# Semaphores between VectorE's two-port operations and GpSimd's adds, all shifts on GpSimd, new buffer rings, and score phases of distinct row groups

## Chip, cores, metric

One core of one Trainium2 chip. The metric is the device time of one execution in microseconds (us), compared in runs of the same chip. The experiments ran in three calls on three chips, each beside the kernel before on the same chip; where kernels of different calls are compared, the ratio to before is the fair measure and a difference of medians is only near it.

## The reference

```python
def _A_ref(x, wq, wk, wv, wo):                    # 32 heads of 16, one shared key/value head
    q = (x @ wq).reshape(B, S, 32, 16).transpose(0, 2, 1, 3)
    k, v = x @ wk, x @ wv                         # S = 2048, D = 512
    p = _softmax(einsum("bhqd,bkd->bhqk", q, k) * 16 ** -0.5)
    return einsum("bhqk,bkd->bhqd", p, v).transpose(0, 2, 1, 3).reshape(B, S, 512) @ wo
# ...
xn = _layernorm(A_x)
s = _A_ref(xn, ...)
g = _silu(silu(xn @ B_w1) @ B_w2)                 # 512 -> 1792 -> 512
return A_x + s * g
```

Attention dominates: 2048 score tiles of 128 keys x 512 queries (32 head groups of 64 tiles) must each pass an exponential and be multiplied by V.

## The kernel before

The kernel plans all engines at build time: a small scheduler places every operation on a modelled clock, and what comes out is one fixed order of instructions per engine, with semaphore waits for data hazards. The chip then runs those orders; only the waits react to real durations.

A score tile is a 32-row matmul. Up to four of them, in four different row groups of the array, form one "score phase" and run side by side. A tile then takes one of two ways.

- Exact: ScalarE computes exp out of PSUM, two neighbouring banks per instruction where it can (128x1024), else one (128x512).
- Approximate: VectorE writes `a*x + b` as uint16, which read as bf16 is a rough exp (Schraudolph's trick). Four such tiles form a batch (`db_sb`). Three more copies of the batch, with 32, 64 and 96 added to the bit patterns (`ds_sb`, the "shifts"), are weighted into V, so that the errors cancel. An approximated tile so costs four products with V instead of one.

Products with V are 32-column matmuls, four side by side (a "round"), accumulated in one PSUM bank. When a head group is complete, VectorE transposes the bank, takes reciprocals and multiplies.

A shift can be done by either engine; the scheduler withdraws the other's task once one is placed:

```python
whole[DV] = pl.add(Task(DV, T_SH, lambda v: v.tensor_scalar(           # 128x2048 uint16
    ds_sb[:, s, :], db_sb[:, bt.b, :], SHIFT[j - 1], 1.0, op0=ALU.add, op1=ALU.mult),
    reads, ds_keys(s), lambda: URGENT if urgent() else 6, list(bt.P.values()),
    on_place=lambda op: placed(op, DV), ports=2,
    gate=lambda: urgent() or len(shifts) >= DV_MIN))                   # DV_MIN = 4
whole[PO] = pl.add(Task(PO, T_P64, lambda g: g.int64_add(              # four uint16 in one word
    ds_sb[:, s, :].bitcast(U64), db_sb[:, bt.b, :].bitcast(U64), words),
    reads, ds_keys(s), lambda: 5 if urgent() else 6, list(bt.P.values()),
    on_place=lambda op: placed(op, PO), ports=2))
```

`ports=2` marks operations that use the pair of SBUF ports that VectorE shares with GpSimd: VectorE's shifts, the normalising multiply (`otr_sb`), the last residual add (`ob_sb`), and every GpSimd add. In the plan they exclude each other, on the chip nothing says so:

```python
def locked(self, eng, ports):
    if ports != 2 or eng not in self.lock:
        return 0.0
    return self.lock[PO if eng == DV else DV]    # end of the other's last one, in the plan only
# ...
NDB, NDS = 7, 6          # batch and shift buffers;  NPA, PRESS = 26, 20: exp tiles
NMIN = 2                 # a score phase may have two matmuls
t3 = pl.add(Task(DV, 332.0, ... v.tensor_tensor(o3, f3, rcp.to_broadcast(...), ALU.mult),
    [("F", k), ("rcp", k)], [("otr", oi % 2, e)], 3, [t2, ...], ports=2))        # priority 3
```

The softmax here doesn't subtract the row's maximum and nothing guards it: scores larger than these inputs give would overflow.

## Time and profile before

| | before |
|---|---|
| time, median of 3 | 695.43 us |
| span of the profiled run | 693.2 us |
| score phases / of them with two matmuls / doubled row groups | 649 / 101 / 14 |
| rounds of 32-column matmuls | 1677 |
| double / single exps | 600 / 148 |
| approximated tiles; shifts on GpSimd / VectorE | 700; 489 / 36 |

The counts below the line are of the built program. The page of the kernel before: first the busy time of each engine with its share and number of instructions, then groups of instructions (line, engine, operation, output <- input, count | busy us, mean ns of one | idle time before, and what ended it).

```profile
PE 670.8 (97%) x8843; PEld 193.8 (28%) x8843; DVE 627.9 (91%) x1088; ACT 667.4 (96%) x827; POOL 519.5 (75%) x500
...
L1341 ACT ACTIVATE pa_sb<-ps 128x1024 bf16<-128x1024 f32 (+1 forms) x748 | 639.7, 980 | 7.4 <-PE ps L776 6.3
L1019 POOL INT64_ADD ds_sb<-db_sb x489 | 515.5, 1072 | 158.9 <-DVE db_sb L962 102.9
L962 DVE TENSOR_SCALAR db_sb<-ps 128x512 uint16<-128x512 f32 x700 | 449.9, 682 | 44.1 <-PE ps L776 40.0
...
L1014 DVE TENSOR_SCALAR ds_sb<-db_sb 128x2048 uint16<-128x2048 uint16 x36 | 37.3, 1039 | 0.1
...
L1100 DVE TENSOR_TENSOR otr_sb<-f_sb,rcp_sb 128x256 bf16<-128x256 f32 x32 | 19.0, 595 | 0.2
```

ScalarE and TensorE are both 96 to 97% busy. A mean can mix two shapes or two situations: start-to-start, a double exp takes 0.904 us and a single one 0.477 when nothing holds it. Split by whether a GpSimd add overlaps them in time, the 36 VectorE shifts took 0.696 us alone (3 of them) and 1.07 beside an add (33, up to 1.60); the multiply 0.417 alone (7) and 0.645 beside an add (25, up to 1.26).

The list of waits of the kernel before (engine, what waited <- for whom: us in total, times, longest). The first line also holds the idle time that the engine shows at every change from rounds to a score phase, 0.425 us in the median of all 649, so only what is longer is lateness:

```profile
PEld ps L776 <- DVE db_sb L962: 104.1, 227, 1.2
POOL ds_sb L1019 <- DVE db_sb L962: 102.9, 69, 34.1
...
POOL ds_sb L1019 <- PE ps L1079: 55.2, 34, 5.3
...
PEld ps L1079 <- DVE ds_sb L1014: 3.2, 5, 1.3
...
PE ps L1079 <- DVE f_sb L1096: 2.8, 6, 0.6
```

### The profile page before, as it was taken

The page shows a single profiled execution, that of the slowest core. Times are in us where ns is not written, and L with a number is a line of the kernel's source. Part 1 is how long each engine was busy: PE and PEld are TensorE (multiplying, and loading weights), DVE is VectorE, ACT ScalarE, POOL GpSimd, SP SyncE. Part 2 cuts the span into 40 slices and gives each one's busy share as a digit, 9 for nine tenths or more (in the row PEclk, how much of TensorE's full clock was granted, in tenths as well). Part 3 has the DMA queues.
Part 4 walks back from the last instruction along what each step waited for, and adds up shares of the span by engine and source line. Part 5 has one row for each costly group of instructions (what it writes and reads, how often), then busy time and mean ns, then how long its engine had stood idle before and what let it go on. Part 6 is the DMA issues. An engine that isn't in the chain of part 4 may idle for free.

```text
span 693.2 us, 20821 instructions
## 1 busy us (share of the span) xinstructions
PE 670.8 (97%) x8843; PEld 193.8 (28%) x8843; DVE 627.9 (91%) x1088; ACT 667.4 (96%) x827; POOL 519.5 (75%) x500
## 2 busy tenths in 40 slices
PE   8899999999999999999999999999999999999995
PEld 4422222222222222222222222222222222222221
DVE  9889989989998999989998999989899988999994
ACT  4899999999999999999999999999999999999994
POOL 2067887797897778877698676788789677888891
PEclk9999999999999999999999999999999999999999
DMA  9310000000000000000000100000000000000000
GB/s 302 127 18 1 3 2 2 1 3 2 2 2 17 18 32 2 2 2 2 1 2 2 32 18 17 1 2 3 2 2 1 17 18 24 9 2 2 2 2 31
DMA packets 11435, 12.64 MB, mean 18 GB/s; under 512 B 1808, under 2 KB 10768, under 8 KB 11344
## 3 DMA queue, kind: packets, MB, share of 16 engines
q1 hardware_dynamic: 10288, 11.28, 5.1%
q8 instruction: 71, 1.16, 0.7%
q10 hardware_dynamic: 1056, 0.03, 0.1%
q14 instruction: 20, 0.16, 0.1%
HBM read 8.95 MB, written 2.10 MB: 16 GB/s over the span
## 4 chain that ended last, share of the span: by engine, by line
PE 62%; ACT 24%; DVE 12%; issue 1%; ACTq 0%; DVEq 0%
PE ps L1079 25%; ACT pa_sb L1341 23%; PE ps L776 21%; PE ps L466 15%; DVE db_sb L962 5%; DVE ds_sb L1014 2%; ACT t_sb L588 1%; DVE stats_sb L413 1%; DVE f_sb L1096 1%; DVE ob_sb L643 1%; DVE u_sb L590 0%; DVE otr_sb L1100 0%; DVE xn_sb L442 0%; DVE fin_sb L640 0%; DVE xnT_sb L493 0%
## 5 line engine op out<-in xcount | busy, mean ns | idle before, releaser
L1341 ACT ACTIVATE pa_sb<-ps 128x1024 bf16<-128x1024 f32 (+1 forms) x748 | 639.7, 980 | 7.4 <-PE ps L776 6.3
L1019 POOL INT64_ADD ds_sb<-db_sb x489 | 515.5, 1072 | 158.9 <-DVE db_sb L962 102.9
L962 DVE TENSOR_SCALAR db_sb<-ps 128x512 uint16<-128x512 f32 x700 | 449.9, 682 | 44.1 <-PE ps L776 40.0
L776 PE MATMUL ps<-qt_sb,kt_sb 32*128 32x512 bf16 x2048 | 257.4, 384 | 9.1 <-DVE db_sb L962 4.0
L1079 PE MATMUL ps<-ds_sb,v_sb 128*32 128x512 bf16 x2100 | 265.1, 383 | 0.2
L1079 PE MATMUL ps<-pa_sb,v_sb 128*32 128x512 bf16 x1348 | 242.8, 383 | 1.8 <-DVE ds_sb L1014 1.0
L1079 PE MATMUL ps<-db_sb,v_sb 128*32 128x512 bf16 x700 | 171.0, 383 | 2.8 <-DVE f_sb L1096 2.8
L776 PEld LDWEIGHTS ps<-qt_sb,kt_sb 32*128 32x128 bf16 x2048 | 63.9, 91 | 281.6 <-ACT pa_sb L1341 145.8
L1079 PEld LDWEIGHTS ps<-ds_sb,v_sb 128*32 128x32 bf16 x2100 | 65.9, 95 | 60.7 <-issue 40.0
L1079 PEld LDWEIGHTS ps<-pa_sb,v_sb 128*32 128x32 bf16 x1348 | 61.2, 95 | 45.1 <-issue 23.6
L466 PE MATMUL ps<-xnT_sb,w_sb 128*32 128x512 bf16 x896 | 73.1, 384 | 0.2 <-DVE db_sb L962 0.2
L466 PE MATMUL ps<-w_sb,u_sb 128*32 128x512 bf16 x896 | 69.6, 384 | 0.0
L1079 PEld LDWEIGHTS ps<-db_sb,v_sb 128*32 128x32 bf16 x700 | 42.6, 95 | 25.8 <-issue 13.3
L588 ACT ACTIVATE t_sb<-ps 128x512 bf16<-128x512 f32 x72 | 46.3, 643 | 0.0
L590 DVE SCALAR_TENSOR_TENSOR u_sb<-t_sb,ps 128x512 bf16<-128x512 bf16 x56 | 38.1, 681 | 4.5 <-ACT t_sb L588 4.0
L1014 DVE TENSOR_SCALAR ds_sb<-db_sb 128x2048 uint16<-128x2048 uint16 x36 | 37.3, 1039 | 0.1
L1096 DVE STREAM_TRANSPOSE f_sb<-ps 128x512 f32<-128x512 f32 x32 | 22.7, 708 | 7.5 <-PE ps L1079 7.4
L466 PEld LDWEIGHTS ps<-xnT_sb,w_sb 128*32 128x32 bf16 x896 | 16.7, 94 | 25.0 <-issue 18.3
L466 PEld LDWEIGHTS ps<-w_sb,u_sb 128*32 128x32 bf16 x896 | 16.2, 94 | 26.3 <-issue 22.8
L466 PE MATMUL ps<-wo_sb,on_sb 128*32 128x512 bf16 x256 | 20.4, 383 | 0.1
L466 PE MATMUL ps<-xnT_sb,wq_sb 128*32 128x512 bf16 x256 | 20.3, 383 | 0.0
L1100 DVE TENSOR_TENSOR otr_sb<-f_sb,rcp_sb 128x256 bf16<-128x256 f32 x32 | 19.0, 595 | 0.2
(53 smaller groups left out, 153.3 us busy)
## 6 DMA issues: line engine op xcount, KB each, us to landing
w_sb<-in_B_w_dram SPq DMA_DIRECT2D x2, 1792.0 KB, 13.1
xr_sb<-in_A_x_dram SPq DMA_DIRECT2D x16, 128.0 KB, 2.6
out_dram<-ob_sb SPq DMA_DIRECT2D x16, 128.0 KB, 1.7
ds_sb<-in_A_x_dram SPq DMA_DIRECT2D x3, 512.0 KB, 7.2
ds_sb<-in_A_x_dram SPq DMA_DIRECT2D x4, 128.0 KB, 2.6
wq_sb<-in_A_wq_dram SPq DMA_DIRECT2D x1, 512.0 KB, 5.2
wo_sb<-in_A_wo_dram SPq DMA_DIRECT2D x1, 512.0 KB, 16.0
kt_sb<-kt_sb SPq DMA_DIRECT2D x4, 64.0 KB, 2.3
```

What stands on the lines that cost most here:

```text
L413: ts_ = pl.add(Task(DV, 593.0, lambda v, t=t: v.bn_stats(stats_sb[:, t, :], x_tile(t)), [xkey(t)], [("st", t)], 1 + j, gate=(lambda: q_don ...
L466: last = h.matmul(bank(b)[32 * j:32 * (j + 1), 0:n], lhsT=lhs(j), rhs=rhs, start=start, stop=stop, tile_position=(0, 32 * j), skip_group_c ...
L588: t1 = Task(AC, 490.0, lambda a: a.activation(t_sb[:, k, :], src, ACT.Tanh, scale=scale), [held], [("t", k)], 0, [t0])
L590: t2 = Task(DV, T_P, lambda v: v.scalar_tensor_tensor(out=dst, in0=t_sb[:, k, :], scalar=1.0, in1=src, op0=ALU.add, op1=ALU.mult), [held, ...
L776: return pe.matmul(bank(b), lhsT=kt_sb[32 * i:32 * i + 32, g % 2, kt * P:(kt + 1) * P], rhs=qt_sb[32 * i:32 * i + 32, (g // 2) % NQR, :], ...
L962: bt.P[i] = pl.add(Task(DV, T_P, lambda v, b=b, i=i, bb=bt.b: v.tensor_scalar(db_sb[:, bb, i * NQ:(i + 1) * NQ], bank(b), 128.0 * LOG2E, 1 ...
L1014: whole[DV] = pl.add(Task(DV, T_SH, lambda v: v.tensor_scalar(ds_sb[:, s, :], db_sb[:, bt.b, :], SHIFT[j - 1], 1.0, op0=ALU.add, op1=ALU.m ...
L1019: whole[PO] = pl.add(Task(PO, T_P64, lambda g: g.int64_add(ds_sb[:, s, :].bitcast(U64), db_sb[:, bt.b, :].bitcast(U64), words), reads, ds_ ...
L1079: h = pe.matmul(bank(OB)[32 * i:32 * (i + 1), :], lhsT=lhs, rhs=rhs, start=s0, stop=s1, tile_position=(0, 32 * i), skip_group_check=True)
L1096: t1 = pl.add(Task(DV, T_TR, lambda v: v.transpose(f_sb[:, k, :], bank(OB)), [("ps", OB)], [("F", k)], 1, [norm.get(("m", g - 2))]))
L1100: t3 = pl.add(Task(DV, 332.0, lambda v: v.tensor_tensor(o3[:, :, val:val + DH], f3[:, :, val:val + DH], rcp_sb[:, k, :].unsqueeze(2).to_br ...
L1341: op = pl.place(AC, 0.8333 * NQ * n + T_AF, lambda a: a.activation(pa_sb[:, s * NQ:(s + n) * NQ].rearrange("p (b n) -> p b n", n=NQ), ps3[ ...
```

## The change

Intent: make the exclusion real with semaphores, so that a two-port operation of one engine never blocks inside the other's; take the shifts off VectorE altogether; let GpSimd stand back when a VectorE two-port operation is about to be ready, and place that one first; and choose the row groups of a score phase distinct, three or four at a time. SBUF moves from exp tiles and batches to shift buffers.

```diff
-T_P64, DV_MIN, T_LIB = 1035.0, 4, 300.0
+T_P64, DV_MIN, T_LIB = 1035.0, 40, 300.0          # 40 is never reached: no VectorE shift
+HOLD_PO, URG_SPLIT = 300.0, 0                     # nor when urgent
-NEAR, AHEAD = 24, 0.6
+NEAR, AHEAD = 12, 0.6
-NPA, PRESS = 26, 20
+NPA, PRESS = 22, 16
+NDB, NDS = 6, 8                                   # were 7, 6
-WIDE, NMIN, EARLY = 2, 2, 200.0
+WIDE, NMIN, EARLY = 2, 3, 200.0
# place(): a real dependency on the other engine's last two-port operation
+        other = self.last2.get(PO if eng == DV else DV) if ports == 2 and eng in self.last2 else None
+        if other is not None:
+            deps.append(other)
# avail(): GpSimd stands back
+        if task.eng == PO and task.ports == 2:
+            for d in self.tasks[DV]:
+                if d.ports == 2 and d.gate is None and all(p.op is not None for p in d.preds) and (
+                        self.ready(DV, d.reads, d.writes) <= self.clk[PO] + HOLD_PO):
+                    return None
# the multiply and the residual add come first
-  [("F", k), ("rcp", k)], [("otr", oi % 2, e)], 3, ...
+  [("F", k), ("rcp", k)], [("otr", oi % 2, e)], -1, ...
# pick_a(): a row group already used in the phase is taken again only if nothing else is left
-  if len(res) < n and a_left(gg, i) > 0 and (i not in used or len(used) == 4 or gg == g and nleft[gg] <= 4):
+  if len(res) < n and a_left(gg, i) > 0 and (i not in used or not strict and not res):
# (cut: release of a batch per quarter, splitting code that stays unused with NPIECE = 1; in the
# plan the exclusion now ends when the other engine can see the semaphore, not when the operation ends)
```

The built program has 657 score phases (1 doubled row group, none of two matmuls), 1676 rounds, 652 double and 32 single exps, 712 approximated tiles and 534 GpSimd adds.

More of the change, by code (lines that the diff above doesn't have):

```diff
@@ L22 @@
 T_P, T_SH, T_TR, T_AF = 600.0, 600.0, 630.0, 64.3
-T_P64, DV_MIN, T_LIB = 1035.0, 4, 300.0
+T_P64, DV_MIN, T_LIB = 1035.0, 40, 300.0
+NPIECE = 1
+HOLD_PO, URG_SPLIT = 300.0, 0
 RSQRT_M = float(0x5F1FFFF9)
@@ L50 @@
 CLOSING, URGENT = 3, 1.5
-NPA, PRESS = 26, 20
+NPA, PRESS = 22, 16
+NDB, NDS = 6, 8
+STOL4 = 0.0
 START_Z, START_H = 8, 14
 EVAC = ()
-WIDE, NMIN, EARLY = 2, 2, 200.0
+WIDE, NMIN, EARLY = 2, 3, 200.0
 ONE_LIMIT = 2500.0
@@ L92, in __init__ @@
         self.dma_t = self.acc_t = 0.0
-        self.lock = {DV: 0.0, PO: 0.0}
+        self.last2 = {DV: None, PO: None}
     def vis(self, op, eng):
@@ L138, in place @@
         op.end = t0 + dur
-        if eng in self.lock and ports == 2:
-            self.lock[eng] = op.end
+        if eng in self.last2 and ports == 2:
+            self.last2[eng] = op
         op.dma, op.ring = dma, None
@@ L161, in locked @@
     def locked(self, eng, ports):
-        if ports != 2 or eng not in self.lock:
+        if ports != 2 or eng not in self.last2:
             return 0.0
-        return self.lock[PO if eng == DV else DV]
+        other = self.last2[PO if eng == DV else DV]
+        return 0.0 if other is None else self.vis(other, eng)
     def add(self, task):
@@ L295, in bass_recurrent_scan__grouped_kv_mqa__dense_activation_silu__prompt_kernel @@
     BANKS = (0, 1, 2, 3, 4, 5, 7)
-    NDB, NDS = 7, 6
     NQR, NON = 4, 2 * NOC
@@ L643, in final @@
             t2 = Task(DV, 333.0, lambda v: v.tensor_tensor(ob_sb[:, tt % 4, :], fin_sb[:, k, :], xr_sb[:, tt % 4, :], ALU.add),
-                      [("fin", k), ("xr", tt % 4)], [("ob", tt % 4)], 1, [t1, xr_task[tt], out_task.get(tt - 4)], ports=2)
+                      [("fin", k), ("xr", tt % 4)], [("ob", tt % 4)], -1, [t1, xr_task[tt], out_task.get(tt - 4)], ports=2)
             t3 = Task(SP, 60.0, lambda e: e.dma_start(of.rearrange("(t p) d -> p t d", p=P)[:, tt, :], ob_sb[:, tt % 4, :]),
@@ L811, in d_batch @@
             bt = Job()
-            bt.g, bt.slots, bt.b, bt.P, bt.nsh, bt.left = g, {}, free[0], {}, 0, K + 3
+            bt.g, bt.slots, bt.b, bt.P, bt.nsh, bt.left = g, {}, free[0], {}, 0, 4 * K
             return bt
@@ L816, in pick_a @@
             res = []
-            used = set()
+            used = set(avoid)
             g = a_group(0)
             st["gA"] = g
-            for gg in (g, g + 1):
-                if gg >= NG:
-                    break
-                order = sorted(range(4), key=lambda i: (i in avoid and gg == g, -a_left(gg, i), i))
-                again = True
-                while len(res) < n and again:
-                    again = False
-                    for i in order:
-                        if len(res) < n and a_left(gg, i) > 0 and (i not in used or len(used) == 4 or gg == g and nleft[gg] <= 4):
-                            if not slot_ok(gg, i):
-                                return None if not res else res
-                            res.append((gg, i, take(gg, i)))
-                            used.add(i)
-                            again = True
+            for strict in (True, False):
+                for gg in (g, g + 1):
+                    if gg >= NG:
+                        break
+                    again = True
+                    while len(res) < n and again:
+                        again = False
+                        for i in sorted(range(4), key=lambda i: (-a_left(gg, i), i)):
+                            if len(res) < n and a_left(gg, i) > 0 and (i not in used or not strict and not res):
+                                if not slot_ok(gg, i):
+                                    return None if not res else res
+                                res.append((gg, i, take(gg, i)))
+                                used.add(i)
+                                again = True
             return res
@@ L854, in s_phase_ready @@
             n = min(n, 4)
-            while n > NMIN and bt[n - 1][0] > need:
+            while n > NMIN and bt[n - 1][0] > need + STOL4:
                 n -= 1
@@ L993, in bass_recurrent_scan__grouped_kv_mqa__dense_activation_silu__prompt_kernel, with ready @@
         shifts = []
-        shifts = []
         def split(bt, s, j):
-            whole = {}
-            def placed(pop, eng):
-                other = DV if eng == PO else PO
-                pl.tasks[other].remove(whole[other])
-                shifts.remove(whole)
-                release(bt)
-                for i in range(4):
+            whole = {"po": []}
+            width = 4 // NPIECE
+            def ready(pop, slots):
+                for i in slots:
+                    release(bt)
                     kt = bt.slots[i]
@@ L1008, in placed, with placed_dv, placed_po @@
                                          [("Ds", s, i)] + v_reads(j, kt), ("s", s)))
+            def placed_dv(pop):
+                for t in whole["po"]:
+                    pl.tasks[PO].remove(t)
+                shifts.remove(whole)
+                ready(pop, range(4))
+            def placed_po(pop, k):
+                if whole[DV] is not None:
+                    pl.tasks[DV].remove(whole[DV])
+                    whole[DV] = None
+                    shifts.remove(whole)
+                ready(pop, range(k * width, (k + 1) * width))
             reads = [("Db", bt.b, i) for i in range(4)]
@@ L1016, in split @@
                 reads, ds_keys(s), lambda: URGENT if urgent() else 6, list(bt.P.values()),
-                on_place=lambda op: placed(op, DV), ports=2,
-                gate=lambda: urgent() or len(shifts) >= DV_MIN))
-            whole[PO] = pl.add(Task(PO, T_P64, lambda g: g.int64_add(
-                ds_sb[:, s, :].bitcast(U64), db_sb[:, bt.b, :].bitcast(U64), words),
-                reads, ds_keys(s), lambda: 5 if urgent() else 6, list(bt.P.values()),
-                on_place=lambda op: placed(op, PO), ports=2))
+                on_place=placed_dv, ports=2, gate=lambda: URG_SPLIT and urgent() or len(shifts) >= DV_MIN))
+            for k in range(NPIECE):
+                cols = slice(k * width * NQ, (k + 1) * width * NQ)
+                whole["po"].append(pl.add(Task(PO, T_P64, lambda g, cols=cols: g.int64_add(
+                    ds_sb[:, s, cols].bitcast(U64), db_sb[:, bt.b, cols].bitcast(U64), words),
+                    reads[k * width:(k + 1) * width], ds_keys(s)[k * width:(k + 1) * width],
+                    lambda: 5 if urgent() else 6, list(bt.P.values()),
+                    on_place=lambda op, k=k: placed_po(op, k), ports=2)))
             shifts.append(whole)
@@ L1102, in make_norm @@
                 rcp_sb[:, k, :].unsqueeze(2).to_broadcast([P, NQ // 32, DH]), ALU.mult),
-                [("F", k), ("rcp", k)], [("otr", oi % 2, e)], 3, [t2, t2_task.get(oi - 2)], ports=2))
+                [("F", k), ("rcp", k)], [("otr", oi % 2, e)], -1, [t2, t2_task.get(oi - 2)], ports=2))
             norm[("m", g)] = t3
```

## The prediction

> **What bounds the kernel now.** Two engines at once. The busy table has ScalarE at 96%, TensorE at 97%, VectorE 91%, GpSimd 75%. From the first exp at 13.1 us to the last at 683.8 (timeline) ScalarE runs back to back: a double-bank exp steps every 0.904 us, a single one or a tanh every 0.477. Minimum steps: 600×0.904 + 148×0.477 + 72×0.477 = 647 us; 23 us of those 671 are stalls. TensorE repeats "score phase, then k rounds of four 32-column matmuls": 0.868 us with two rounds, 0.217 for each more, so 0.435 for a score phase with its two mode switches. 649 phases, 1677 rounds and 14 doubled row groups make about 648 us; stalls again 23 us. By the list of waits the largest excess of TensorE's idle time is behind VectorE: late Schraudolph evictions 8 us, transpose 3.4, VectorE shifts 2, gating 1.4.
>
> VectorE is late partly because of collisions: a VectorE shift takes 0.696 us alone, 1.07 mean (up to 1.6) while a GpSimd shift runs; the normalising multiply 0.417 alone, 0.645 beside one, up to 1.26. GpSimd adds take 1.039 alone and 1.19 beside two-port VectorE work. This agrees with the Trainium skill, "SBUF — State Buffer", Who interferes with whom: the second op on the shared port pair fully blocks.
>
> **What the change does** (instruction counts of the built programs).
> - VectorE: 36 shifts leave (37.3 us), 12 evictions come (+7 us); 48 multiplies and adds wait on a semaphore instead of blocking inside. Net −30 to −35 us of occupancy.
> - GpSimd: 489→534 adds, +45×1.02 = +46 us, less the 16 us lost to collisions; about 80% busy.
> - ScalarE: double exps 600→652, singles 148→32: +47.0 −55.3 = −8.3 us.
> - TensorE: 649→657 score phases (+3.5 us), doubled row groups 14→1 (−2.8), rounds 1677→1676. Net +0.5 us.
>
> **Critical path.** ScalarE's demand falls to 639 us, TensorE's stays at 648, so TensorE becomes the sole limit. The gain is what TensorE's 23 us of stalls lose, of which about 15 lie behind VectorE. I expect 7 to 11 us of them to go: VectorE is lighter and never surprised by a blocked shift; ScalarE is nearly 9 us looser. The rest stays: PSUM holds only about two phases ahead, so the mix of two-, three- and four-round cycles still makes each engine wait for the other. Start (13 us) and tail (11 us) hardly move.
>
> **Predicted time: 686 us** (−1.4%), 8 in 10 between 677 and 694. Faster by over 2%: 0.20; within 2%: 0.78; slower by over 2%: 0.02.
>
> **What would show it.** Right: the normalising multiply at 0.42 mean and the output add near 0.41, no spread; every GpSimd add at 1.04; VectorE busy near 590 us; ScalarE busy near 650–655 with more idle before exp; TensorE still 97%, its excess waits behind evictions about 4 us. Wrong: VectorE idle before the multiplies on GpSimd of more than 15 us, passed on to score phases; GpSimd above 90%; TensorE waiting for shifts where VectorE no longer helps; exp waiting for free ring slots (22 instead of 26).
>
> **What would make it wrong.** If TensorE's stalls come from the alternation with ScalarE and not from late VectorE work, little is gained (about 692). If plan and chip agree so much better that stalls nearly vanish, it is near 677. If the semaphores chain a VectorE delay into GpSimd and back, it is no faster.

## More of the kernel before

The evictions (L962), which read PSUM, took 0.682 beside adds and 0.683 alone.

GpSimd waits for work or for a free shift buffer, and for no two-port operation of VectorE: there is no semaphore to wait for.

## The result

| | before | after |
|---|---|---|
| time, median of 4 | 695.49 us | 685.14 us |
| ratio, 95% interval | 1 | 0.9849 [0.9832, 0.9866] |
| span of the profiled run | 693.2 | 684.2 |
| first exp / last exp end / span end | 13.1 / 683.8 / 693.2 | 13.3 / 674.8 / 684.2 |
| TensorE excess over minimum cycles | 24.3 | 12.4 |
| ScalarE excess over minimum steps | 23.2 | 22.1 |

Ratios here and below are the mean time of one kernel's fast runs over that of the other's of the same rounds, so not quite the ratio of the medians. "TensorE excess" sums, over all score phases, the time to the next one less 0.868 us (two rounds) less 0.217 for each further round (rounds counted in the trace, four matmuls to a round). Doubled row groups are in it: at an estimated 0.217 each, 3.0 of the 24.3 and 0.2 of the 12.4. "ScalarE excess" sums start-to-start steps from the first exp to the last, less 0.904 (double exp) and 0.477 (single exp, tanh).

The page of the changed kernel:

```profile
PE 668.1 (98%) x8887; PEld 191.7 (28%) x8887; DVE 603.0 (88%) x1064; ACT 658.8 (96%) x763; POOL 548.8 (80%) x545
...
L1042 POOL INT64_ADD ds_sb<-db_sb x534 | 544.9, 1040 | 117.8 <-DVE db_sb L975 65.2
L1365 ACT ACTIVATE pa_sb<-ps 128x1024 bf16<-128x1024 f32 (+1 forms) x684 | 630.5, 1027 | 6.8 <-PE ps L789 6.3
L975 DVE TENSOR_SCALAR db_sb<-ps 128x512 uint16<-128x512 f32 x712 | 468.6, 684 | 61.4 <-PE ps L789 57.7
...
L1124 DVE TENSOR_TENSOR otr_sb<-f_sb,rcp_sb 128x256 bf16<-128x256 f32 x32 | 13.3, 417 | 0.3
```

The multiply now takes 0.417 on average, and GpSimd's adds 1.040. ScalarE runs 684 exps where it ran 748. The list of waits of the changed kernel:

```profile
PEld ps L789 <- DVE db_sb L975: 80.0, 178, 0.7
...
POOL ds_sb L1042 <- DVE db_sb L975: 65.2, 48, 32.5
...
POOL ds_sb L1042 <- DVE otr_sb L1124: 32.3, 29, 2.2
POOL ds_sb L1042 <- PE ps L1103: 10.4, 13, 2.8
POOL ds_sb L1042 <- DVE ob_sb L656: 9.3, 10, 1.1
```

The new lines are the third and the fifth: GpSimd waits 32.3 us for the multiply and 9.3 us for the residual add. VectorE hardly waits for GpSimd at all. TensorE's wait behind evictions fell from 104.1 us in 227 waits to 80.0 in 178; taking 0.43 off each wait that is longer than 0.46, the excess fell from 8.2 to 4.2 us. By the same count, over PEld and PE together, the waits before rounds behind the transpose fell from 2.6 to 1.1 and those behind VectorE's shifts from 1.7 to nothing.

### The profile page after: what moved, and what is told of

It reads as the page before. It is cut to its first block, busy times and chain, and to the rows that moved or that the text cites. A ratio compares the mean times of both kernels' runs of the same rounds, so it can differ in the third digit from the quotient of the medians.

```text
span 684.2 us, 21033 instructions
## 1 busy us (share of the span) xinstructions
PE 668.1 (98%) x8887; PEld 191.7 (28%) x8887; DVE 603.0 (88%) x1064; ACT 658.8 (96%) x763; POOL 548.8 (80%) x545
## 4 chain that ended last, share of the span: by engine, by line
PE 54%; ACT 35%; DVE 9%; issue 1%; DMA 1%; SPq 0%; DVEq 0%
ACT pa_sb L1365 33%; PE ps L1103 22%; PE ps L789 19%; PE ps L479 14%; DVE db_sb L975 4%; ACT t_sb L601 2%; DVE stats_sb L426 1%; DVE f_sb L1120 1%; DVE u_sb L603 1%; DMA ds_sb<-in_A_x_dram 1%; DVE xn_sb L455 0%; DVE otr_sb L1124 0%; DVE xnT_sb L506 0%; DVE tmp_sb L603 0%; SPq L373 0%
## 5 line engine op out<-in xcount | busy, mean ns | idle before, releaser
L1042 POOL INT64_ADD ds_sb<-db_sb x534 | 544.9, 1040 | 117.8 <-DVE db_sb L975 65.2
L1365 ACT ACTIVATE pa_sb<-ps 128x1024 bf16<-128x1024 f32 (+1 forms) x684 | 630.5, 1027 | 6.8 <-PE ps L789 6.3
L975 DVE TENSOR_SCALAR db_sb<-ps 128x512 uint16<-128x512 f32 x712 | 468.6, 684 | 61.4 <-PE ps L789 57.7
L1103 PE MATMUL ps<-ds_sb,v_sb 128*32 128x512 bf16 x2136 | 277.5, 383 | 0.0
L1103 PE MATMUL ps<-db_sb,v_sb 128*32 128x512 bf16 x712 | 186.5, 384 | 1.1 <-DVE f_sb L1120 1.1
L1103 PEld LDWEIGHTS ps<-ds_sb,v_sb 128*32 128x32 bf16 x2136 | 69.1, 95 | 54.0 <-issue 35.3
L479 PE MATMUL ps<-w_sb,u_sb 128*32 128x512 bf16 x896 | 73.1, 384 | 0.0
L1103 PEld LDWEIGHTS ps<-db_sb,v_sb 128*32 128x32 bf16 x712 | 46.3, 95 | 22.3 <-issue 14.5
L1124 DVE TENSOR_TENSOR otr_sb<-f_sb,rcp_sb 128x256 bf16<-128x256 f32 x32 | 13.3, 417 | 0.3
L603 DVE SCALAR_TENSOR_TENSOR tmp_sb<-t_sb,ps 128x512 bf16<-128x512 bf16 x16 | 10.8, 677 | 2.0 <-ACT t_sb L601 1.9
```

Of the source, the lines that this page charges most:

```text
L479: last = h.matmul(bank(b)[32 * j:32 * (j + 1), 0:n], lhsT=lhs(j), rhs=rhs, start=start, stop=stop, tile_position=(0, 32 * j), skip_group_c ...
L603: t2 = Task(DV, T_P, lambda v: v.scalar_tensor_tensor(out=dst, in0=t_sb[:, k, :], scalar=1.0, in1=src, op0=ALU.add, op1=ALU.mult), [held, ...
L975: bt.P[i] = pl.add(Task(DV, T_P, lambda v, b=b, i=i, bb=bt.b: v.tensor_scalar(db_sb[:, bb, i * NQ:(i + 1) * NQ], bank(b), 128.0 * LOG2E, 1 ...
L1042: whole["po"].append(pl.add(Task(PO, T_P64, lambda g, cols=cols: g.int64_add(ds_sb[:, s, cols].bitcast(U64), db_sb[:, bt.b, cols].bitcast( ...
L1103: h = pe.matmul(bank(OB)[32 * i:32 * (i + 1), :], lhsT=lhs, rhs=rhs, start=s0, stop=s1, tile_position=(0, 32 * i), skip_group_check=True)
L1124: t3 = pl.add(Task(DV, 332.0, lambda v: v.tensor_tensor(o3[:, :, val:val + DH], f3[:, :, val:val + DH], rcp_sb[:, k, :].unsqueeze(2).to_br ...
```

## The experiments

Twelve kernels, five rounds each against the kernel before on the same chip. The medians of before were 695.15, 694.93 and 695.74. The expectations weigh four theories: 1, late VectorE work cost the time; 2, the new choice of score phases and exps is the gain; 3, the semaphores themselves are; 4, found on the way, the semaphores help because they move the wait to GpSimd. Code cuts are shortened where they say so or end in dots. All results agreed with the reference within its tolerance.

### Semaphores alone, on both orders

Adding or removing only the dependency leaves the order of every engine exactly as it was, since the plan's clock had the exclusion already. First, the kernel before with it:

```diff
+        other = self.last2.get(PO if eng == DV else DV) if ports == 2 and eng in self.last2 else None
+        if other is not None:
+            deps.append(other)
```

> The kernel before with the mutual semaphores alone: the order of every engine is exactly that of before, only waits are added. Theory 1 (TensorE lost time behind late VectorE work; the exclusion in itself is only a move of the same wait from inside the instruction to in front of it): collisions vanish from the durations (multiply 0.42, VectorE shift 0.70 to 0.93, GpSimd add 1.04), but the waits stand before the instructions, so 693 to 699 us. Theory 3 (the semaphores themselves are the gain, because a blocked two-port operation costs more than a wait): 687 to 691 us.

Measured: 691.55 us, ratio 0.9947 [0.9935, 0.9960]. Theory 1's range was missed on the good side and theory 3's upper end was nearly met: 3.6 us came from waits alone. The collisions are gone (multiply 0.423, shift 0.691, add 1.038). VectorE waits for adds 8.4 us in front of its shifts and 5.4 in front of the multiply; GpSimd waits 26.4, 13.7 and 6.4 us for shifts, multiplies and residual adds. Two lines of its page, and GpSimd's list of waits:

```profile
L1019 DVE TENSOR_SCALAR ds_sb<-db_sb 128x2048 uint16<-128x2048 uint16 x36 | 24.8, 691 | 8.7 <-POOL ds_sb L1024 8.4
...
L1105 DVE TENSOR_TENSOR otr_sb<-f_sb,rcp_sb 128x256 bf16<-128x256 f32 x32 | 13.5, 423 | 6.1 <-POOL ds_sb L1024 5.4
```

```profile
POOL ds_sb L1024 <- DVE ds_sb L1019: 26.4, 29, 1.8
POOL ds_sb L1024 <- DVE otr_sb L1105: 13.7, 20, 1.9
POOL ds_sb L1024 <- DVE ob_sb L648: 6.4, 9, 1.1
```

Second, the changed kernel without the dependency:

```diff
-        if other is not None:
-            deps.append(other)
```

> The changed kernel without the mutual semaphores; the order of every engine is exactly that of the changed kernel. Theory 1: no VectorE shifts are left and the plan keeps the multiplies apart from the adds, so few collide and the time is within 2 us of the changed kernel, 684 to 688. Theory 3: collisions come back (multiply mean over 0.55) and 5 us or more are lost, 690 to 695.

Measured: 694.27 us, ratio 0.9980 [0.9967, 0.9993]. Theory 1 fails clearly here. The four kernels make a table of medians:

| | no semaphores | semaphores |
|---|---|---|
| order of before | 695.15 | 691.55 |
| order of after | 694.27 | 685.14. It was run at another time. |

The new order by itself is worth 0.9 us, the semaphores 3.6 on the old order and 9.1 on the new; the ratios, 0.9980 against 0.9849, give the same 9.1. TensorE's excess, summed as above, goes the same way: 24.3 to 20.7 us on the old order, 20.0 to 12.4 on the new. The two-port groups of the kernel without semaphores:

```profile
L1122 DVE TENSOR_TENSOR otr_sb<-f_sb,rcp_sb 128x256 bf16<-128x256 f32 x32 | 25.3, 791 | 0.1
...
L654 DVE TENSOR_TENSOR ob_sb<-fin_sb,xr_sb 128x512 bf16<-128x512 bf16 x16 | 10.4, 663 | 0.0
```

Together 25.3 + 10.6 us by summed durations, where the changed kernel needs 13.3 + 6.7: VectorE is blocked for 15.9 us. One case, seen first on VectorE and then on GpSimd (start us, length us, engine, line, operation, count, idle before <- releaser):

```profile
174.89 0.23 DVE L1121 RECIPROCAL rcp_sb<-f_sb 128x16 f32<-128x16 f32 x1
175.30 0.69 DVE L973 TENSOR_SCALAR db_sb<-ps 128x512 uint16<-128x512 f32 x1 [0.18 <-PE ps L787]
175.91 1.34 DVE L1122 TENSOR_TENSOR otr_sb<-f_sb,rcp_sb 128x256 bf16<-128x256 f32 x1
177.17 1.95 DVE L973 TENSOR_SCALAR db_sb<-ps 128x512 uint16<-128x512 f32 x3
```

```profile
173.90 3.07 POOL L1040 INT64_ADD ds_sb<-db_sb  x3
177.65 1.04 POOL L1040 INT64_ADD ds_sb<-db_sb  x1 [0.68 <-PE ps L1101]
```

The view starts at 174 and shows the last three adds of a row of 18 that runs without a gap from 158.70. The multiply begins at 175.91, in the last 0.05 us of the second of these three, and is held through the third: it takes 1.34 us and ends 0.28 after it. This is the longest case. Of the 22 multiplies of this run that began during an add and were held, 20 ended some 0.28 us after that one add, and two, which began just before its end, after the next. The same multiply in the changed kernel:

```profile
173.27 0.23 DVE L1123 RECIPROCAL rcp_sb<-f_sb 128x16 f32<-128x16 f32 x1
173.68 0.69 DVE L975 TENSOR_SCALAR db_sb<-ps 128x512 uint16<-128x512 f32 x1 [0.18 <-PE ps L789]
174.29 0.42 DVE L1124 TENSOR_TENSOR otr_sb<-f_sb,rcp_sb 128x256 bf16<-128x256 f32 x1
174.62 1.49 DVE L975 TENSOR_SCALAR db_sb<-ps 128x512 uint16<-128x512 f32 x2
```

```profile
171.31 2.05 POOL L1042 INT64_ADD ds_sb<-db_sb  x2
174.80 4.09 POOL L1042 INT64_ADD ds_sb<-db_sb  x4 [1.45 <-DVE otr_sb L1124]
```

Here GpSimd stays idle for 1.45 us until the multiply is through, and VectorE loses nothing. The waiting time has not vanished; it has moved from VectorE to GpSimd. This is the new theory, number 4.

### Is it the order "multiply first"?

Only GpSimd waits, VectorE does not; the order is kept:

```diff
-        if other is not None:
+        if other is not None and eng == PO:
             deps.append(other)
```

> The changed kernel, order of every engine kept, with only half of the mutual semaphores: a GpSimd add still waits for the two-port VectorE operation planned before it, but a VectorE operation no longer waits for the add before it. Theory 4 (the semaphores help because the add is held until the multiply is through, so the wait lies on GpSimd): as the changed kernel, 684 to 687, multiply mean under 0.46 us. If the VectorE side of the exclusion is what helps: like the kernel without semaphores, 691 to 695.

Measured: 684.82 us, ratio 0.9845 [0.9831, 0.9858], the same as the changed kernel. One two-port operation in 48 overlapped an add. GpSimd waits as before:

```profile
POOL ds_sb L1042 <- DVE otr_sb L1124: 32.5, 29, 2.3
...
POOL ds_sb L1042 <- DVE ob_sb L656: 9.2, 10, 1.1
```

So all of the semaphores' gain on the new order comes from holding the add back. The other half of the exclusion is worth nothing measurable there. The opposite half, with VectorE alone waiting, was not run.

### Which engine's lateness costs?

Four kernels add work to one engine of the changed kernel, with the order of everything else kept.

```diff
# TensorE: 38 score phases, evenly spread, issued twice (shortened, as are the next three)
+            row[k].emit = lambda pe, f=f: (f(pe), f(pe))[1]
```

> The changed kernel, order of every engine kept, with 38 score phases issued twice (idempotent), evenly spread: 38 x 0.217 = 8.2 us more TensorE work. The changed kernel measured 685.1. If TensorE is the sole limit of the changed kernel, as predicted: 692 to 694, nearly all of it shows. If ScalarE and TensorE still bind alike: 688 to 691.

```diff
# ScalarE: 18 more exps, SBUF to a scratch tile
+            op.emit = lambda e: e.activation(pad_sb[:], zer_sb[:], ACT.Exp)
```

> The changed kernel, order kept, with 18 single-bank exps to a scratch tile added to ScalarE, evenly spread: about 18 x 0.48 = 8.6 us of ScalarE work. If ScalarE really has some 8 us of slack against TensorE: 686 to 690, half of it or less shows. If the slack cannot be used because each engine holds only two phases ahead: 691 to 694.

```diff
# VectorE: three scratch reciprocals before each reciprocal in front of a multiply
+            lambda v, m=m: v.reciprocal(pad_sb[:, m, :], f_sb[:, k, :] ... ) for m in range(3)
```

> The changed kernel, order kept, with three scratch reciprocals (0.154 us each) before each of the 32 normalising multiplies: 14.8 us of VectorE work at the places where the kernel without semaphores loses 16 us in blocked multiplies. If the semaphores help because they keep lateness off VectorE (new theory 4: the wait is moved to GpSimd, which has slack): 689 to 695, like the kernel without semaphores (694.3). If the blocked multiplies cost something other than VectorE time: 685 to 687.

```diff
# GpSimd: 30 half-size adds to a scratch tile, each in front of a real one
+            lambda g: g.int64_add(pad_sb[:].bitcast(U64), db_sb[:, b, 0:2 * NQ].bitcast(U64), words)
```

> The changed kernel, order kept, with 30 half-size adds to a scratch tile put in front of evenly spread GpSimd adds: about 30 x 0.5 = 15 us of GpSimd work. Theory 4 (GpSimd has slack, its lateness is absorbed by the ring of 8 shift buffers): 685 to 687. If GpSimd's lateness reaches TensorE: 688 or more.

| extra work on | added (start to start) | time | change against 685.14 | ratio to before | change by the ratios |
|---|---|---|---|---|---|
| TensorE | 8.2 us (38 x 0.217, an estimate) | 692.58 | +7.4 | 0.9964 [0.9952, 0.9977] | +8.0 |
| ScalarE | 9.4 us (18 x 0.524) | 691.28 | +6.1 | 0.9950 [0.9936, 0.9963] | +7.0 |
| VectorE | 12.1 us (96 x 0.126) | 688.94 | +3.8 | 0.9910 [0.9896, 0.9923] | +4.2 |
| GpSimd | 17.6 us (30 x 0.587) | 685.27 | +0.1 | 0.9859 [0.9845, 0.9872] | +0.7 |

(The changed kernel itself stood at 0.9849 of before, in another call, so the last column, in us of 695.5, is the fairer; each of its values is uncertain by about 1.5 us.) The VectorE pads came out at 0.126 us instead of the 0.154 expected, so 12.1 us were added and not 14.8; its result lies just below the range that theory 4 gave. Two things follow. ScalarE still binds: two thirds to three quarters of its extra work show, against nine tenths or more for TensorE. TensorE's result alone lies in the range that was given for a sole limit (692 to 694); it is ScalarE's, above the 686 to 690 that slack would have given, that speaks against one. And a microsecond of lateness on VectorE costs about 0.3, one on GpSimd nothing measurable. This fits the finding that it pays to let GpSimd wait, but it does not account for all of it. The blocked multiplies and residual adds cost more for their size, 9.1 us for 15.9 (0.57 each), where the rate of the pads would give an estimated 5. They come in lumps of up to 0.9 us and behind residual adds as well, where the pads are an even 0.38 per head group; whether that is the reason was not tested and stays open.

### Were the VectorE shifts the burden?

The kernel before, order kept, its 36 VectorE shifts cut to 64 of 2048 columns. Most of those shifts' values are then stale or missing; the outcome still passed the tolerance.

```diff
-                ds_sb[:, s, :], db_sb[:, bt.b, :], SHIFT[j - 1], 1.0, op0=ALU.add, op1=ALU.mult),
+                ds_sb[:, s, 0:64], db_sb[:, bt.b, 0:64], SHIFT[j - 1], 1.0, op0=ALU.add, op1=ALU.mult),
```

> The kernel before, same order, with the 36 VectorE shifts cut from 2048 to 64 columns (wrong result on purpose). It takes some 30 us of VectorE time and most of the collisions with GpSimd away and changes nothing else. Theory 1: TensorE's excess falls by 5 to 10 us, time 686 to 691. Theory 2 (the gain is the new plan's fuller score phases and double exps, late VectorE matters little): within 2 us of before, 693.5 to 696.

Measured: 692.00 us, ratio 0.9948 [0.9935, 0.9961]: between the two theories, 3.2 us. The shifts took 17.0 us together instead of 37.4. They did not shrink to 0.18 us, because 32 of 36 still met an add and were blocked. So 20.4 us less on VectorE gave 3.2 us.

Then the kernel before, replanned without VectorE shifts and nothing else:

```diff
-T_P64, DV_MIN, T_LIB = 1035.0, 4, 300.0
+T_P64, DV_MIN, T_LIB = 1035.0, 40, 300.0
-                gate=lambda: urgent() or len(shifts) >= DV_MIN))
+                gate=lambda: len(shifts) >= DV_MIN))
```

> The kernel before, replanned with no shift on VectorE (all 534 on GpSimd), nothing else changed: old rings, old choice of score phases, 654 phases and 1689 rounds, which is 6 us more TensorE demand than before (5 phases x 0.435, 13 more doubled rows x 0.217, 12 rounds x 0.217, less overlap between the two). Theory 1: the relief of VectorE outweighs it, 687 to 693 us. Theory 2: no gain or a loss, 695 to 702 us.

Measured: 711.98 us, ratio 1.0235 [1.0222, 1.0248]. Both theories missed it; taking the shifts off VectorE alone is a loss of 17 us. Two places show why. At the end, GpSimd still has a queue of adds when the last exp is done (at 691.3). The view starts at 688; the row without a gap is one of 30 adds, from 669.61:

```profile
687.04 13.22 POOL L1019 INT64_ADD ds_sb<-db_sb  x13
```

They end at 700.3, so the span from the last exp to the end is 18.8 us where it was 9.4. And in the middle, one multiply:

```profile
356.99 6.65 DVE L1100 TENSOR_TENSOR otr_sb<-f_sb,rcp_sb 128x256 bf16<-128x256 f32 x1
363.57 0.68 DVE L962 TENSOR_SCALAR db_sb<-ps 128x512 uint16<-128x512 f32 x1
```

```profile
354.21 9.16 POOL L1019 INT64_ADD ds_sb<-db_sb  x9
```

```profile
359.43 0.65 ACT L588 ACTIVATE t_sb<-ps 128x512 bf16<-128x512 f32 x1
364.96 1.02 ACT L1341 ACTIVATE pa_sb<-ps 128x1024 bf16<-128x1024 f32 x1 [4.87 <-PE ps L776]
```

The view of GpSimd starts at 355 and shows the last nine of a row of 30 adds that runs without a gap from 332.88 to 363.37. The multiply, begun at 356.99, gets through only after the last of them: 6.65 us, beside seven adds. VectorE's evictions stop, no bank comes free, and ScalarE then sits idle for 4.87 us behind a score phase.

### A ladder from before to after

Step 2: the kernel before with semaphores, without VectorE shifts and with the new rings, all three together.

```diff
 # b_sem and b_noshift together, and:
-NPA, PRESS = 26, 20
+NPA, PRESS = 22, 16
-    NDB, NDS = 7, 6
+    NDB, NDS = 6, 8
```

> A ladder between the two kernels: before + mutual semaphores + no shift on VectorE + the new rings (8 shift, 6 batch, 22 exp buffers); score phases still chosen as before (104 of two matmuls, 14 doubled rows, 666 phases, 1660 rounds: 2 us more TensorE demand than before with semaphores, by 17 x 0.435 - 17 x 0.217 - 3). If the old ring of 6 is what made no-shift-on-VectorE lose 17 us (GpSimd 9 us behind at the end): the tail after the last exp is back to 9.4 us and the time is 688 to 694. If no-shift in itself is bad: over 697.

Measured: 690.63 us, ratio 0.9927 [0.9915, 0.9940], in the range for the ring. The tail from the last exp is 9.4 us again. As the semaphores came in with the rings, the run does not separate the two against the 711.98; the tail of queued adds is the part that a deeper ring explains, and that part is argued, not shown by itself. The plan also approximates fewer tiles here, 692 instead of 700.

Step 3: also the new choice of score phases (`pick_a`, `NMIN = 3`, `NEAR = 12`), which leaves out of the change `HOLD_PO`, the two priorities and, in the plan's clock, the moment at which the exclusion ends.

> The next step of the ladder: also score phases of three or four matmuls with distinct row groups (651 phases, 1680 rounds, 7 us less TensorE demand than the step before less 4 of rounds, so about -3 to -5 with the doubled rows). It differs from the changed kernel only in that GpSimd is not held for a ready VectorE multiply and the multiply keeps its old low priority. Theory 2 (fuller phases are part of the gain): 4 to 8 us below the step before, 683 to 688, so close to the changed kernel. If the hold and the priority carry the gain: 689 or more.

Measured: 683.65 us, ratio 0.9830 [0.9816, 0.9844]. The step is worth 7.0 us. TensorE's excess falls from 15.2 to 12.2 us, of which the doubled row groups (14 to 3) are an estimated 2.4. But the step is a new plan, and fuller phases (651 instead of 666) are not all that it changes: 28 more tiles are approximated (720 instead of 692), 685 exps run instead of 697, and by the steps of 0.904 and 0.477 ScalarE's minimum falls by an estimated 12.6 us. How much of the 7.0 belongs to which was not tested. And it is not slower than the changed kernel, so no gain of the hold and the priorities is to be seen on top of the semaphores; a small one could be hidden, since the changed kernel's plan asks an estimated 3.4 us more of ScalarE and 1.3 more of TensorE. Without them VectorE waits only 2.0 us for adds in front of the multiply, GpSimd 15.8 us for multiplies.

| step | time | ratio to before | in us of 695.5 |
|---|---|---|---|
| before | 695.15 | 1 | |
| + semaphores | 691.55 | 0.9947 | -3.7 |
| + no VectorE shift, + rings | 690.63 | 0.9927 | -5.1 |
| + new choice of score phases | 683.65 | 0.9830 | -11.8 |
| + hold, priorities = the change | 685.14 | 0.9849 | -10.5 |

The last two differ by less than their intervals. Each step from the second on is a new plan, so a difference between steps is in part a matter of how the plan happens to fall, as the counts of tiles above show.

### A version that beats both

In the changed kernel GpSimd's last add ends 7.5 us before the last exp does, while ScalarE and TensorE still bind. Two constants let the last head group use approximated tiles longer and shorten a wait of the rounds. The two were not run one by one.

```diff
-MARGIN, MARGIN_END = 16, 28
+MARGIN, MARGIN_END = 16, 20
-HOLD, Q_LEAD = 1000.0, 3.3
+HOLD, Q_LEAD = 600.0, 3.3
```

> A candidate that should beat both: the changed kernel with two constants altered: approximated tiles are still taken in the last head group down to 20 left instead of 28 (in the changed kernel GpSimd ends 7.5 us before the last exp), and a weighted-sum round waits at most 0.6 us for a missing row group instead of 1.0. Counts: 651 phases, 1682 rounds (TensorE -1.3 us), 640 double and 44 single exps (ScalarE -5.1 us). As ScalarE and TensorE both still bind (+8 us on either showed as +7 and +6), I expect 1 to 4 us less than the changed kernel: 681 to 684.

Measured: 681.93 us, ratio 0.9802 [0.9789, 0.9815], 3.2 us below the median of the changed kernel, with intervals that do not touch.

## Why the prediction was right, and where not

The time (686 predicted, 685.14 measured) and the range held. Point by point:

- "I expect 7 to 11 us of [TensorE's stalls] to go". Right in place and size: TensorE's excess fell by 11.9 us, or 9.1 without the doubled row groups that the prediction had counted as work.
- "TensorE becomes the sole limit". Wrong. 9.4 us more on ScalarE cost 6.1 us, 8.2 us more on TensorE 7.4 (7.0 and 8.0 by the ratios). ScalarE's own excess hardly moved (23.2 to 22.1), so on its row the gain is nearly the 8.3 us of exps that became double or were approximated. Both engines gained about the same, one by doing less and one by waiting less.
- "VectorE is lighter and never surprised by a blocked shift" as one cause. This mixed two things that the runs separate. Lighter: 20.4 us off VectorE's shifts gave 3.2 us, and moving all shifts to GpSimd gave nothing without the other parts (a loss of 17 us alone). Not blocked: this was the larger part, 9.1 us on the new order.
- "48 multiplies and adds wait on a semaphore instead of blocking inside". Wrong engine: in the changed kernel GpSimd waits (32.3 and 9.3 us) and VectorE does not. The prediction counted the semaphores as a rearranged VectorE wait, and so left out of its sum why they pay.
- VectorE busy "near 590": 603.0. Evictions overlap less: 393 of 712 begin before the instruction ahead has ended, where 508 of 700 did. One that follows another so steps by 0.598 us, while a record by itself lasts 0.683, so the busy time overstates the work that is left. ScalarE busy "650 to 655": 658.8. GpSimd "about 80%": 80%. Evictions' excess "about 4 us": 4.2. The start and tail, "hardly move": 13.1 to 13.3 us, and 9.4 both times (not the 11 that the prediction gave the tail), right.
- The new choice of score phases was counted by its demand alone (+0.5 us on TensorE, -8.3 on ScalarE, "nearly 9 us looser") and got no share of the gain by name. In the ladder the step that brings it in is worth 7.0 us, more approximated tiles included.

So the total was right in part by luck: two understated terms, the semaphores and the replanned score phases, stood against an overstated one, the relief of VectorE by moved shifts.

The Trainium skill was used in two places. "SBUF — State Buffer", section Who interferes with whom, says that the shared pair is an exclusive lock on which the second comer blocks, and that a VectorE instruction with at most one SBUF input outside the two-port modes does not contend. Both agree with this trace: multiplies at 0.645 against 0.417, evictions out of PSUM at 0.682 beside adds and 0.683 alone. The same section says "Issue order, not op shape, decides who blocks": the changed kernel turns that into a tool, by a semaphore that puts the multiply first.

## What to carry to other kernels

Where two engines share a resource, decide by semaphore which of them waits, and let it be the one whose lateness the measurement shows to be free (here only this way round was run); a plan that merely assumes the exclusion loses it on the chip. Find that engine by adding a known amount of work to each in a fixed order, rather than from busy shares: 98% and 96% busy engines both bound here, one at 88% cost 0.3 per microsecond, one at 80% nothing. And test parts of a change in combination: here one part alone lost 17 us and another gained 3.6 or 9.1 depending on the order around it. And count what a replanned step moves besides the thing that it is named after.

## What the Trainium skill lacked or had wrong

- "SBUF — State Buffer", Summary: rules for kernel authors, says that the second comer blocks until the first instruction finishes. Most held multiplies here agree: in the changed order without semaphores 20 of 22 ended 0.28 us after the add that they met. Against a row of GpSimd adds issued back to back it can be longer: one multiply of 0.417 us, in the kernel before without VectorE shifts, stood for 6.65 us, through seven adds to the end of the row. Why that one case was so much longer was not tried.
- The same page's summary advises to schedule whichever is off the critical path. It does not say how to see which that is, or that a semaphore can enforce it: 9.1 us between the same orders with and without it, all of it kept when only GpSimd waits.
- No page has a duration for GpSimd's 64-bit integer add (it would belong to "GPSIMD Engine Reference", Performance versus the Vector engine): four packed uint16 per word over 128x2048 took 1.040 us in the records and 1.015 start to start, where VectorE's own shift took 0.696 alone.
